# Scans with a PSUM operand, other first tiles and another order of a tile's matmul groups in a fused attention and expert kernel

## The chip, the core and the metric

The kernel runs on one core of one Trainium2 chip. The metric is the device time of one execution in microseconds (us). PE is TensorE (PEld its weight loads), DVE is VectorE, ACT is ScalarE, POOL is GpSimd, SP is SyncE, which issues nearly all DMAs.

## The reference

Three layers follow one another. The first is attention with a decaying state, for 4 batches, 8 heads, 768 steps and 48 channels:

```python
for t in range(S):
    state = alpha[:, :, t, :, None] * state + np.einsum('bhd,bhe->bhde', k[:, :, t], v[:, :, t])
    y[:, :, t] = np.einsum('bhd,bhde->bhe', q[:, :, t], state)
```

Its 3072 rows of 384 numbers then go through a mixture of eight experts: each row goes to the expert with the highest cosine similarity to `expert_emb` (divided by `tau`) and is weighted by the softmax's share of that expert. A dense layer with ELU (384 to 2048 to 384) ends the program. All of it is float32.

## The kernel before

**Tiles.** Attention runs over 24 tiles, numbered i: six chunks of 128 steps, and in each chunk the four batches. A tile holds all eight heads as four pairs (`NP`); a pair's two heads of 48 channels lie on partitions 0 to 47 and 64 to 111 (`C2` = 112 rows). The decays of a tile (`at`) are one row of four segments of `TP` = 129 values, 517 in all (`SW`). Four `at` and four `qk` buffers and five `vt` buffers rotate, so tile i + 4 is loaded into the buffer of tile i. The code works as follows; lines are those of the profile.

- `stR` (L340): one DVE scan from right to left gives R, the product of the decays from each step to the tile's end. Its second operand `back` is a row in SBUF that holds a floor, and 1.0 at each segment's end. A reciprocal (L341) puts 1/R of each segment's first step into the row `fore`. POOL makes Kh = k times R (L343).
- `stA` (L350): a second scan, of `at` with `fore`, gives A, the inverse factor of each step. POOL makes Qh = q times A (L352).
- `stS` (L380), "scores": 16 matmuls of Kh and Qh, 48 rows each, into two PSUM tiles. `stP` (L387): DVE multiplies each of the two with a triangle, which gives P.
- `stT` (L364): four transposes of Kh, copied by ACT to Kt (L367).
- `stC`: from chunk 1 on 16 matmuls of the carried state G with Qh ("state's share", L402, 48 rows by 64 columns); 16 of v with P ("values", L405, 128 rows by 64 columns), both into the one PSUM tile psY, which ACT copies to yT (L407); from chunk 1 on two matmuls with the identity that carry G over (L412); and 16 of Kt with v ("state's products", L415, 128 by 64) which make the next state. In the last chunk there is no next state, so L364, L412 and L415 are missing for tiles 20 to 23.
- `stG` copies the new state out of PSUM (ACT, L423), `stH` scales it by the tile's decay (ACT, four of L433).
- `stD` (L446): eight matmuls with `rhsX` give the tile's rows and the products with the normalized expert embeddings; ACT copies them (L459) and sums squares (L462), DVE reduces the products (L451, kept in the list `late`).
- Routing: six `GROUPS` of tiles go through some 29 small DVE instructions each (`stR1`, `stX`, `gates`, `stR2`), handed out twelve to a tile from the list `todo`; rows are then scaled by ACT and scattered by POOL's indirect DMA (`put`, L556).

**Order.** `fast()` is written out by hand (`manual_schedule`): each engine executes its instructions in the order of the code. In iteration i of the loop PE gets: scores of i + 1, transposes of i + 1, `stD` of i - 1, state's share, values, carry, state's products of i. DVE gets R of i + 2, P of i + 1 (first half), A of i + 2, P of i + 1 (second half), then small instructions. ACT gets the copies in the order in which the code names them, with `stE` (L356, a copy of eight values of A that waits for the scan) ahead of the copy of psY.

**Start.** Before the loop, SP issues the loads of tiles 0 to 3, of v for three tiles, of the constants, of `emb` (after tile 1) and of `sel`. PE multiplies ones eleven times (`warm`, L285), and tiles 0 and 1 are prepared. The embeddings' inverse norm is 11 small DVE instructions in `todo`; the scaled embeddings (L675) are transposed (L725, eT) in iteration 1, ahead of the first `stD`, which therefore is done for tiles 0 and 1 together in iteration 2.

After the loop, `ending()` finishes tiles 22 and 23, routes the last groups, and the experts' layers (`moe1`, L956 on) and the dense layer (`moe2`, L1144 on) follow; the change touches neither.

PSUM has eight banks: two for psX, three for the scores and the new state (psG), and one each for psT, psY and psR.

Of the kernel before, what the change touches and what calls it, by code (L numbers as in the profile page):

```python
# [8 lines left out]
F32 = mybir.dt.float32  # L9
# [17 lines left out]
TP = T + 1  # L27
SW = H // 2 * TP + 1
# [20 lines left out]
A_FLOOR = 1e-15  # L49
# [12 lines left out]
def fused_kernel(ctx, tc, qk, a, v, emb, w12, wi, wo, cst, sel, cols, out):  # L62
# [64 lines left out]
    def inv_norm1(pool, x):  # L127

        shape = [x.shape[0], 1]
        y = pool.tile(shape, F32, name="rs_y1")  # L130
        t = pool.tile(shape, F32, name="rs_t1")
        h = pool.tile(shape, F32, name="rs_h1")
        yi = y.bitcast(I32)
        steps = [
            lambda: nc.vector.tensor_scalar(yi, x.bitcast(I32), 1, None, op0=ALU.logical_shift_right),
            lambda: nc.vector.tensor_scalar(h, x, -0.5, None, op0=ALU.mult),
            lambda: nc.vector.tensor_scalar(yi, yi, -1.0, float(0x5F3759DF), op0=ALU.mult, op1=ALU.add),
        ]
# [5 lines left out]
        steps += [  # L144
            lambda: nc.vector.tensor_scalar(y, y, x, 1e-6, op0=ALU.mult, op1=ALU.add),
            lambda: nc.vector.reciprocal(y, y),
        ]
        return y, steps

# [137 lines left out]
    def attention():  # L287
        with ExitStack() as st:
# [15 lines left out]
            back = gp.tile([C2, SW], F32, name="back")  # L304
            fore = [gp.tile([C2, SW], F32, name=f"fore{i}") for i in range(2)]
# [4 lines left out]

            def seg(t, n=TP):

                return t[:, :NP * TP].rearrange("c (p t) -> c p t", t=TP)

# [17 lines left out]
            def stR(i):  # L332
# [10 lines left out]
                nc.gpsimd.tensor_tensor(Kh[i], qkt[i][:, 1], R[:, 1:].rearrange("c (p t) -> c p t", t=TP)[:, :, 1:], op=ALU.mult)  # L343

            def stA(i):
# [4 lines left out]
                nc.vector.tensor_tensor_scan(A, at.pop(i), fore[i % 2], 0.0, op0=ALU.mult, op1=ALU.add)  # L350
                Qh[i] = wk.tile([C2, NP, T], F32, bufs=3, name="Qh")
                nc.gpsimd.tensor_tensor(Qh[i], qkt.pop(i)[:, 0], seg(A)[:, :, 1:], op=ALU.mult)  # L352

            def stE(i):
                if i < NT:
                    nc.scalar.activation(out=chk[:, i], in_=seg(As.pop(i))[:, :, 0:TP:T], func=AF.Copy)  # L356

# [31 lines left out]
            yT = {}  # L389

            def stC(i):
                if i < 0 or i >= NT:
                    return
                cc, b = divmod(i, B)
                vv = vt[i % VB]
                y = psG.tile([128, NP, T], F32, tag="g", name="psY") if i == NT - 1 else ps1.tile([128, NP, T], F32, name="psY")
                pp, qh = P.pop(i), Qh.pop(i)
                if cc:
                    for p in range(NP):
                        for h2 in range(2):  # L400
                            rows = slice(HP * h2, HP * h2 + D)
                            nc.tensor.matmul(y[HP * h2:HP * (h2 + 1), p], G[b][rows, p], qh[rows, p], start=(p == 0), stop=False)  # L402
                for p in range(NP):
# [4 lines left out]
                if cc < NC - 1:  # L408
                    u = psG.tile([C2, NP, D], F32, tag="g", name="psU")
                    kk = Kt.pop(i)  # L410
                    if cc:
                        nc.tensor.matmul(u, c["ident"][:C2, :C2], G[b][:, :, :D], start=True, stop=False)  # L412
# [3 lines left out]
                    U_[i] = u  # L416
# [8 lines left out]
            def stH(i):  # L425
# [4 lines left out]
                if i >= B:  # L430
                    g = G[i % B]
                    for p in range(NP):
                        nc.scalar.activation(out=g[:, p, :D], in_=g[:, p, :D], func=AF.Copy, scale=seg(r)[:, p, 1:2])  # L433
# [5 lines left out]
            def stD(i, keep=False):  # L439
# [4 lines left out]
                x = psD.tile([128, NP, 128], F32, name="psX")  # L444
# [73 lines left out]

            def stR2(g):
# [3 lines left out]
                r = ps1.tile([128, 8, E], F32, tag="psT" if g == NG - 2 else "psR", name="psR")[:, :n]  # L523
# [50 lines left out]
            def general():  # L574
# [15 lines left out]
                with tc.For_i(0, NC, 1) as cc, tc.For_i(0, T // TB, 1) as tb:  # L590
                    ts = bass.ds(tb * TB, TB)
                    for b in range(B):
                        for p in range(NP):
                            for h2 in range(2):
                                p0 = (b * H + 2 * p + h2) * EG
                                ch = slice(h2 * HP, h2 * HP + D)
                                for nm, src in (("a", a[bass.ds(cc, 1), ch, b, bass.ds(tb * TB + (p * TP + 1), TB)]),
# [38 lines left out]
            def fast():  # L636
# [14 lines left out]
                warm(ps1, "psY", 11)  # L651
                nc.scalar.activation(out=warm_t, in_=ones, func=AF.Exp)
                nc.vector.memset(back, A_FLOOR)
                nc.vector.memset(back[:, 1:].rearrange("c (p t) -> c p t", t=TP)[:, :, T:], 1.0)
                nc.vector.memset(cum[:, 0], 0.0)
                for t in fore + G:
                    nc.gpsimd.memset(t, 0.0)
                zero = xp.tile([128, 1, XW], F32, tag="xt", name="zero")
                nc.gpsimd.memset(zero, 0.0)
                for j in range(2):  # L660
                    stR(j)
                    stA(j)
                    stE(j)
                    stH(j)
                rows, rtau = emb_t[:, :2 * NP * HP], emb_t[:, 2 * NP * HP:]
                es = sm.tile([E, 1], F32, name="es")
                esq = wk.tile([E, 2 * NP * HP], BF16, bufs=1, tag="junk", name="esq")
                nc.scalar.activation(out=esq, in_=rows, func=AF.Square, accum_out=es)
                en, steps = inv_norm1(sm, es)
                stS(0)  # L670
                stT(0)
# [624 lines left out]
```

## Time and profile before

| | |
|---|---|
| median of 3 runs | 808.1 us (806.57 to 811.5) |
| the profiled execution | 807.42 us |
| its span in the trace | 805.6 us |
| busy, share of the span: PE, DVE, ACT, POOL | 96%, 67%, 44%, 24% |

Times in the trace are counted from the span's start. What is called S0 to S23 below is the start of PE's weight loads for the scores of that tile (L380): each marks a tile. A wait is printed behind an instruction in brackets, with its length and what ended it.

### The profile page before, as it was taken

The page shows a single profiled execution, that of the slowest core. Times are in us where ns is not written, and L with a number is a line of the kernel's source. Part 1 is how long each engine was busy: PE and PEld are TensorE (multiplying, and loading weights), DVE is VectorE, ACT ScalarE, POOL GpSimd, SP SyncE. Part 2 cuts the span into 40 slices and gives each one's busy share as a digit, 9 for nine tenths or more (in the row PEclk, how much of TensorE's full clock was granted, in tenths as well). Part 3 has the DMA queues.
Part 4 walks back from the last instruction along what each step waited for, and adds up shares of the span by engine and source line. Part 5 has one row for each costly group of instructions (what it writes and reads, how often), then busy time and mean ns, then how long its engine had stood idle before and what let it go on. Part 6 is the DMA issues. An engine that isn't in the chain of part 4 may idle for free.

```text
span 805.6 us, 13707 instructions
## 1 busy us (share of the span) xinstructions
PE 774.2 (96%) x5064; PEld 700.7 (87%) x5064; DVE 538.6 (67%) x1015; ACT 358.0 (44%) x783; POOL 190.1 (24%) x218
## 2 busy tenths in 40 slices
PE   7799998889999999999999999999999999999996
PEld 5688877669999999999988899999999999999996
DVE  7779999956877788888467665454545545545442
ACT  2466877624554555555355443333333333323331
POOL 6433656612333343343000020010002002002002
PEclk7899999999999999999999999999999999999999
DMA  9988863266656557563000010000001001000001
GB/s 246 255 237 216 229 182 95 109 196 157 194 184 206 179 193 231 173 213 111 1 0 1 2 40 1 0 11 31 1 1 39 1 1 40 0 1 30 11 1 39
DMA packets 44805, 77.72 MB, mean 96 GB/s; under 512 B 11958, under 2 KB 18230, under 8 KB 44734
## 3 DMA queue, kind: packets, MB, share of 16 engines
q1 hardware_dynamic: 41662, 67.36, 28.9%
q0 software_dynamic: 3072, 9.45, 3.2%
q8 instruction: 40, 0.66, 0.4%
q14 instruction: 31, 0.25, 0.1%
HBM read 64.58 MB, written 12.22 MB: 95 GB/s over the span
## 4 chain that ended last, share of the span: by engine, by line
PE 39%; issue 30%; DVE 3%; POOL 2%; ACT 2%; POOLq 0%; ACTq 0%
PE h L1144 6%; PE y L988 5%; PE y L990 4%; PE y L989 4%; PE h L957 4%; PE h L958 4%; PE h L956 4%; POOL out_dram L1178 2%; PE o L1167 2%; PE o L1165 2%; PE o L1166 2%; PE t L937 1%; DVE dlo L260 1%; DVE g L1150 1%; DVE mn L1146 1%
## 5 line engine op out<-in xcount | busy, mean ns | idle before, releaser
L1146 DVE TENSOR_SCALAR mn<-h 128x512 f32<-128x512 f32 x96 | 66.2, 690 | 139.7 <-PE h L1144 139.7
L1147 ACT ACTIVATE mn<-mn 128x512 f32<-128x512 f32 x96 | 60.7, 633 | 171.9 <-DVE mn L1146 171.9
L1167 PE MATMUL o<-dwo,gl 128*128 128x384 f32 x384 | 129.4, 337 | 1.4 <-DVE gl L1154 1.4
L1166 PE MATMUL o<-dlo,gh 128*128 128x384 f32 x384 | 128.4, 334 | 0.0
L1165 PE MATMUL o<-dwo,gh 128*128 128x384 f32 x384 | 128.2, 334 | 0.0
L1144 PE MATMUL h<-xh,dwi 128*128 128x512 f32 x288 | 112.8, 391 | 0.6 <-ACT x2T L1002 0.6
L1144 PE MATMUL h<-xh,dlo 128*128 128x512 f32 x288 | 113.2, 393 | 0.0
L1144 PE MATMUL h<-xl,dwi 128*128 128x512 f32 x288 | 112.5, 392 | 0.0
L1178 POOL DMA_INDIRECT out_dram<-ob,ids x24 | 23.2, 966 | 341.8 <-ACT ob L1175 338.1
L1153 ACT ACTIVATE gh<-g 128x512 fp32r<-128x512 f32 x96 | 60.7, 633 | 77.6 <-DVE g L1150 77.6
L960 ACT ACTIVATE hh<-h 128x432 fp32r<-128x432 f32 (+6 forms) x64 | 32.4, 507 | 106.2 <-PE h L958 99.1
L204 DVE TENSOR_TENSOR wlo<-raw,whi 128x512 fp32r<-128x512 f32 x96 | 73.2, 789 | 5.6 <-ACT whi L201 4.8
L1150 DVE SCALAR_TENSOR_TENSOR g<-mn,h 128x512 f32<-128x512 f32 x96 | 66.1, 688 | 15.2 <-ACT mn L1147 14.7
L1165 PEld LDWEIGHTS o<-dwo,gh 128*128 128x128 f32 x384 | 72.0, 187 | 4.2
L1166 PEld LDWEIGHTS o<-dlo,gh 128*128 128x128 f32 x384 | 72.0, 187 | 4.0
L1167 PEld LDWEIGHTS o<-dwo,gl 128*128 128x128 f32 x384 | 72.2, 188 | 2.1 <-DVE gl L1154 1.7
L961 DVE SCALAR_TENSOR_TENSOR hl<-h,hh 128x432 fp32r<-128x432 f32 (+6 forms) x64 | 36.7, 573 | 47.6 <-ACT hh L960 46.2
L988 PE MATMUL y<-hh,whi 128*128 128x432 f32 (+6 forms) x192 | 68.4, 356 | 0.0
L956 PE MATMUL h<-xh,whi 128*128 128x432 f32 (+6 forms) x192 | 66.5, 346 | 0.7 <-ACTq L1015 0.7
L244 POOL TENSOR_SCALAR dg<-dg 128x384 f32<-128x384 f32 x32 | 42.0, 1312 | 106.3 <-ACT dg L243 106.2
L1154 DVE TENSOR_TENSOR gl<-g,gh 128x512 fp32r<-128x512 f32 x96 | 65.7, 684 | 1.2 <-ACT gh L1153 1.1
L958 PE MATMUL h<-xh,wlo 128*128 128x432 f32 (+6 forms) x192 | 66.4, 346 | 0.0
(210 smaller groups left out, 1520.5 us busy)
## 6 DMA issues: line engine op xcount, KB each, us to landing
raw<-in_w_dram SPq DMA_DIRECT2D x96, 256.0 KB, 3.3
qk<-in_qk_dram SPq DMA_DIRECT2D x40, 192.0 KB, 3.9
vt<-in_v_dram SPq DMA_DIRECT2D x24, 256.0 KB, 4.7
raw<-in_wi_dram SPq DMA_DIRECT2D x16, 384.0 KB, 4.3
raw<-in_wo_dram SPq DMA_DIRECT2D x16, 384.0 KB, 4.1
xr<-xs SPq DMA_DIRECT2D x7, 576.0 KB, 4.9
at<-in_alpha_dram SPq DMA_DIRECT2D x40, 96.9 KB, 3.0
xs<-zero SPq DMA_DIRECT2D x7, 288.8 KB, 5.5
```

The lines of the kernel that those rows point to most:

```text
L204: nc.vector.tensor_tensor(l[:, sl], r, h[:, sl].bitcast(F32), op=ALU.subtract)
L956: nc.tensor.matmul(ps, wh, xh[:, kk], start=(kk == 0), stop=False)
L958: nc.tensor.matmul(ps, wl, xh[:, kk], start=False, stop=(kk == KD - 1))
L988: nc.tensor.matmul(acc[e][d], wh, hh, start=(f == 0), stop=False)
L1144: nc.tensor.matmul(ps, l, x, start=(n == 0), stop=(n == len(terms) - 1))
L1146: nc.vector.tensor_scalar(mn, ps, 0.0, None, op0=ALU.min)
L1147: nc.scalar.activation(out=mn, in_=mn, func=AF.Exp)
L1150: nc.vector.scalar_tensor_tensor(g, mn, -1.0, ps, op0=ALU.add, op1=ALU.max)
L1154: low.append(lambda: nc.vector.tensor_tensor(gl, g, gh.bitcast(F32), op=ALU.subtract))
L1165: nc.tensor.matmul(o_, gh[:, sl], wh, start=(f == 0), stop=False)
L1166: nc.tensor.matmul(o_, gh[:, sl], wl, start=False, stop=False)
L1167: nc.tensor.matmul(o_, gl[:, sl], wh, start=False, stop=(f == M - 1))
```

## The change

**PSUM operand.** One PSUM bank `pz` is set aside; its first column holds the floor (2^-50 in place of 1e-15), and both scans take it, broadcast along the row, as their second operand; `back` and `fore` are gone. Each segment gets three leading values (0, 1/floor, 1) and a trailing 1/floor, so that the scan comes to 1 by itself; a tile's row is 528 values long. The reciprocal goes into the third leading value of `at`. Since psR has no bank any more, its users move: eT and the counts of the first groups to psX, the count of group 4 stays in psT, the last one and the check's sum go into `pz`.

**First tiles.** `emb` is loaded ahead of tile 1. There are 20 warm matmuls and 4 more behind the transposes of tile 0. The inverse norm is split: two DVE instructions (`first`), 14 on ACT (`steps`), a DVE reciprocal in iteration 0 between P and A, and two scalings on ACT; eT follows in iteration 0, and `stD` of tile 0 in iteration 1. Three bf16 constants are made in iteration 3, on ACT and POOL, and no longer ahead of the loop on DVE.

**Order.** `stC` is cut in three: `stC_state` (L402), `stC_carry` (the tile psU and L412) and `stC_values` (L405, L407, L415). PE's order in iteration i becomes: scores of i + 1, state's share of i, transposes of i + 1, `stD` of i - 1, carry of i, values of i, state's products of i. Where `stR2` is due, the reductions in `late` come ahead of it.

The diff, cut to its core:

```diff
+LEAD = 3
+TP = LEAD + T + 1
+SW = NP * TP
...
-A_FLOOR = 1e-15
+A_FLOOR = 2.0 ** -50
@@ inv_norm1 @@
+        first = [
+            lambda: vec.tensor_scalar(yi, x.bitcast(I32), 1, None, op0=ALU.logical_shift_right),
+            lambda: vec.tensor_scalar(yi, yi, -1.0, float(0x5F3759DF), op0=ALU.mult, op1=ALU.add),
         ]
+        steps = [lambda: act.activation(out=h, in_=x, func=AF.Copy, scale=-0.5)]
         for _ in range(3):
             steps += [
-                lambda: nc.vector.scalar_tensor_tensor(t, y, h, y, op0=ALU.mult, op1=ALU.mult),
-                lambda: nc.vector.scalar_tensor_tensor(y, t, 1.5, y, op0=ALU.add, op1=ALU.mult),
+                lambda: act.activation(out=t, in_=y, func=AF.Copy, scale=h),
+                lambda: act.activation(out=t, in_=t, func=AF.Copy, scale=y),
+                lambda: act.activation(out=t, in_=t, func=AF.Copy, bias=1.5),
+                lambda: act.activation(out=y, in_=t, func=AF.Copy, scale=y),
             ]
+        steps += [lambda: act.activation(out=y, in_=y, func=AF.Copy, scale=x, bias=1e-6)]
@@ attention @@
-            back = gp.tile([C2, SW], F32, name="back")
-            fore = [gp.tile([C2, SW], F32, name=f"fore{i}") for i in range(2)]
+            pz_p = st.enter_context(tc.tile_pool(name="pz", bufs=1, space=PS))
+            pz = pz_p.tile([128, 512], F32, name="pz")
+            floor = pz[:C2, 0:1].to_broadcast([C2, SW])
@@ stR, stA @@
-                nc.vector.tensor_tensor_scan(R[:, ::-1], at[i][:, ::-1], back[:, ::-1], 0.0, op0=ALU.mult, op1=ALU.max)
-                nc.vector.reciprocal(seg(fore[i % 2])[:, :, 0:1], seg(R)[:, :, 1:2])
+                nc.vector.tensor_tensor_scan(R[:, ::-1], at[i][:, ::-1], floor, A_FLOOR, op0=ALU.mult, op1=ALU.max)
+                nc.vector.reciprocal(seg(at[i])[:, :, LEAD - 1:LEAD], seg(R)[:, :, LEAD:LEAD + 1])
...
-                nc.vector.tensor_tensor_scan(A, at.pop(i), fore[i % 2], 0.0, op0=ALU.mult, op1=ALU.add)
+                nc.vector.tensor_tensor_scan(A, at.pop(i), floor, 0.0, op0=ALU.mult, op1=ALU.max)
@@ stC @@
             def stC(i):
+
+                stC_state(i)
+                stC_carry(i)
+                stC_values(i)
...
+                if cc < NC - 1:
+                    U_[i] = psG.tile([C2, NP, D], F32, tag="g", name="psU")
+                    if cc:
+                        nc.tensor.matmul(U_[i], c["ident"][:C2, :C2], G[b][:, :, :D], start=True, stop=False)
@@ stR2 @@
-                r = ps1.tile([128, 8, E], F32, tag="psT" if g == NG - 2 else "psR", name="psR")[:, :n]
+                r = count_tile(g)[:, :n]
@@ fast, before the loop @@
                 load(0)
                 nc.sync.dma_start(out=cs, in_=cst)
+                nc.sync.dma_start(out=emb_t, in_=emb)
                 load(1)
                 load_v(0)
-                nc.sync.dma_start(out=emb_t, in_=emb)
...
-                warm(ps1, "psY", 11)
+                warm(ps1, "psY", 20)
...
+                nc.vector.memset(pz[:, 0:1], A_FLOOR)
...
                 for j in range(2):
                     stR(j)
                     stA(j)
-                    stE(j)
                     stH(j)
+                    if j == 0:
+                        stE(j)
+                        nc.scalar.activation(out=esq, in_=rows, func=AF.Square, accum_out=es)
                 stS(0)
                 stT(0)
+                warm(ps1, "psY", 4)
+                for f in guess:
+                    f()
+                nc.vector.reciprocal(rtau, rtau)
+                stE(1)
                 stP(0, 0)
                 stP(0, 1)
-                todo.extend([lambda: nc.vector.reciprocal(rtau, rtau)] + steps
-                            + [lambda: nc.vector.tensor_scalar(rows, rows, en, rtau, op0=ALU.mult, op1=ALU.mult)])
-                nc.vector.tensor_tensor(strict16, c["tri"], c["ident"], op=ALU.subtract)
-                nc.vector.tensor_copy(ident16, c["ident"])
-                nc.vector.tensor_copy(base16[:, 0], c["base"])
+                for f in newton:
+                    f()
@@ the loop @@
                     stS(i + 1)
+                    stC_state(i)
                     stT(i + 1)
                     if i - 3 in last:
+                        while late:
+                            late.pop(0)()
                         todo[:0] = stR2(last[i - 3])
                     stR(i + 2)
                     stP(i + 1, 0)
+                    if i == 0:
+                        nc.vector.reciprocal(en, en)
+                        nc.scalar.activation(out=rows, in_=rows, func=AF.Copy, scale=en)
+                        nc.scalar.activation(out=rows, in_=rows, func=AF.Copy, scale=rtau)
                     stA(i + 2)
                     stP(i + 1, 1)
...
-                    if i == 2:
-                        stD(0)
-                    if i > 1:
+                    if i > 0:
                         stD(i - 1)
+                    stC_carry(i)
                     stE(i + 2)
-                    stC(i)
-                    if i == 1:
-                        step(len(todo))
-                        eT = ps1.tile([128, NP, E], F32, tag="psR", name="eT")
+                    stC_values(i)
+                    if i == 0:
+                        eT = psD.tile([128, NP, E], F32, tag="psX", name="eT")
                         for p in range(NP):
                             nc.tensor.transpose(eT[:, p], rows[:, p * 128:(p + 1) * 128], c["ident"][:E, :E])
-                        nc.vector.tensor_copy(rhsX[:, :, CW:CW + E], eT)
+                        nc.scalar.activation(out=rhsX[:, :, CW:CW + E], in_=eT, func=AF.Copy)
+                    if i == 3:
+                        nc.scalar.activation(out=ident16, in_=c["ident"], func=AF.Copy)
+                        nc.scalar.activation(out=base16[:, 0], in_=c["base"], func=AF.Copy)
+                        nc.gpsimd.tensor_tensor(strict16, c["tri"], c["ident"], op=ALU.subtract)
```

## Rows read from the trace of the kernel before

**Rows 1.** Windows by stage: stretch, busy us of each engine (instructions), PEclk, DMA, GB/s.

```profile
0.00:45.49 45.49, 34.42 (x345) 28.15 (x345) 34.49 (x60) 16.86 (x49) 21.90 (x26) 0.81 0.95 247
45.49:147.04 101.55, 95.35 (x1310) 80.71 (x1308) 95.57 (x198) 71.79 (x228) 56.12 (x59) 1.00 0.66 186
...
171.95:805.60 633.65, 623.91 (x3247) 578.04 (x3246) 386.73 (x625) 258.13 (x473) 100.91 (x113) 1.00 0.22 70
```

**Rows 2.** Timeline of PE's weight loads over one tile: start us, length us, instruction.

```profile
45.49 0.97 PEld L380 LDWEIGHTS psS<-Qh,Kh 48*128 48x128 f32 x16
46.58 0.39 PEld L364 LDWEIGHTS psT<-cs,Kh 112*128 112x128 f32 x4
46.93 0.97 PEld L446 LDWEIGHTS psX<-rhsX,yT 128*128 128x128 f32 x8
48.00 0.85 PEld L402 LDWEIGHTS psY<-Qh,G 48*64 48x64 f32 x16
49.02 0.85 PEld L405 LDWEIGHTS psY<-P,vt 128*64 128x64 f32 x16 [0.17 <-issue]
50.05 0.27 PEld L412 LDWEIGHTS psU<-G,cs 112*112 112x112 f32 x2 [0.17 <-issue]
50.56 0.54 PEld L415 LDWEIGHTS psU<-vt,Kt 128*64 128x64 f32 x16 [0.24 <-issue]
51.15 0.30 PEld L380 LDWEIGHTS psS<-Qh,Kh 48*128 48x128 f32 x4
```

**Rows 3.** The same timeline, tiles 0 and 1 of L446 behind one another.

```profile
28.09 3.53 PEld L446 LDWEIGHTS psX<-rhsX,yT 128*128 128x128 f32 x16
```

**Rows 4.** Timeline of DVE and POOL in the tile of rows 2.

```profile
46.69 0.69 DVE L387 TENSOR_TENSOR P<-psS,cs 128x512 f32<-128x512 f32 x1 [1.26 <-PE psS L380]
47.29 1.23 DVE L350 TENSOR_TENSOR_SCAN A<-at,fore 112x517 f32<-112x517 f32 x1
48.44 0.67 DVE L387 TENSOR_TENSOR P<-psS,cs 128x512 f32<-128x512 f32 x1
48.66 1.19 POOL L352 TENSOR_TENSOR Qh<-qk,A 112x512 f32<-112x512 f32 x1 [2.14 <-DVE A L350]
...
49.11 1.83 DVE L340 TENSOR_TENSOR_SCAN R<-at,back 112x517 f32<-112x517 f32 x1
```

**Rows 5.** DVE's groups from 45.49 to 147.04 us: count | busy us, mean ns | idle.

```profile
L350 DVE TENSOR_TENSOR_SCAN A<-at,fore 112x517 f32<-112x517 f32 x17 | 31.5, 1852 | 0.0
...
L340 DVE TENSOR_TENSOR_SCAN R<-at,back 112x517 f32<-112x517 f32 x16 | 20.9, 1306 | 0.0
```

**Rows 6.** Timeline of DVE and POOL at the start.

```profile
4.00 1.23 DVE L340 TENSOR_TENSOR_SCAN R<-at,back 112x517 f32<-112x517 f32 x1 [2.20 <-DMA at<-in_alpha_dram]
...
7.72 2.10 POOL L352 TENSOR_TENSOR Qh<-qk,A 112x512 f32<-112x512 f32 x1
```

**Rows 7.** Timeline of PE's weight loads, three waits.

```profile
9.87 1.78 PEld L380 LDWEIGHTS psS<-Qh,Kh 48*128 48x128 f32 x16 [4.81 <-POOL Qh L352]
...
25.12 0.32 PEld L725 LDWEIGHTS eT<-cs,emb_t 8*128 8x128 f32 x4 [3.38 <-DVE emb_t L675]
...
145.98 0.97 PEld L446 LDWEIGHTS psX<-rhsX,yT 128*128 128x128 f32 x8 [1.49 <-ACT yT L407]
```

**Rows 8.** One window of 4 us at the start, columns as in rows 1.

```profile
8.00:12.00 4.00, 2.13 (x17) 1.91 (x18) 2.79 (x4) 0.82 (x3) 4.00 (x3) 0.54 1.10 271
```

**Rows 9.** Timeline of DVE: a product with both operands in SBUF.

```profile
79.32 0.65 DVE L204 TENSOR_TENSOR wlo<-raw,whi 128x512 fp32r<-128x512 f32 x1
```

**Rows 10.** ACT's groups from 45.49 to 147.04 us, columns as in rows 5.

```profile
L433 ACT ACTIVATE G<-G,R 112x48 f32<-112x48 f32 x71 | 17.7, 323 | 0.0
L407 ACT ACTIVATE yT<-psY 128x512 f32<-128x512 f32 x17 | 10.0, 591 | 5.9 <-PE psY L405 5.8
...
L356 ACT ACTIVATE chk<-A 112x8 f32<-112x8 f32 x17 | 3.5, 205 | 10.5 <-DVE A L350 10.5
```

**Rows 11.** The DMA view of the first 40 us: GB/s in 40 slices.

```profile
GB/s 0 14 246 305 282 315 297 279 274 281 247 283 342 302 252 285 282 215 186 237 259 225 207 262 246 217 271 360 344 292 253 241 333 287 260 192 265 177 164 262
```

More of the change, by code (lines that the diff above doesn't have):

```diff
@@ L394, in stC @@
                 cc, b = divmod(i, B)
-                vv = vt[i % VB]
-                y = psG.tile([128, NP, T], F32, tag="g", name="psY") if i == NT - 1 else ps1.tile([128, NP, T], F32, name="psY")
-                pp, qh = P.pop(i), Qh.pop(i)
+                y = ys[i] = psG.tile([128, NP, T], F32, tag="g", name="psY") if i == NT - 1 else ps1.tile([128, NP, T], F32, name="psY")
+                qh = Qh.pop(i)
                 if cc:
@@ L402, in stC, with stC_carry, stC_values @@
                             nc.tensor.matmul(y[HP * h2:HP * (h2 + 1), p], G[b][rows, p], qh[rows, p], start=(p == 0), stop=False)
+            def stC_carry(i):
+                if i < 0 or i >= NT:
+                    return
+                cc, b = divmod(i, B)
+                if cc < NC - 1:
+                    U_[i] = psG.tile([C2, NP, D], F32, tag="g", name="psU")
+                    if cc:
+                        nc.tensor.matmul(U_[i], c["ident"][:C2, :C2], G[b][:, :, :D], start=True, stop=False)
+            def stC_values(i):
+                if i < 0 or i >= NT:
+                    return
+                cc, b = divmod(i, B)
+                vv, pp, y = vt[i % VB], P.pop(i), ys.pop(i)
                 for p in range(NP):
@@ L408, in stC @@
                 if cc < NC - 1:
-                    u = psG.tile([C2, NP, D], F32, tag="g", name="psU")
+                    u = U_[i]
                     kk = Kt.pop(i)
-                    if cc:
-                        nc.tensor.matmul(u, c["ident"][:C2, :C2], G[b][:, :, :D], start=True, stop=False)
                     for p in range(NP):
@@ L432, in stH @@
                     for p in range(NP):
-                        nc.scalar.activation(out=g[:, p, :D], in_=g[:, p, :D], func=AF.Copy, scale=seg(r)[:, p, 1:2])
+                        nc.scalar.activation(out=g[:, p, :D], in_=g[:, p, :D], func=AF.Copy, scale=seg(r)[:, p, LEAD:LEAD + 1])
             xt, lg = {}, {}
@@ L443, in stD @@
                 y = yT.pop(i)
-                x = psD.tile([128, NP, 128], F32, name="psX")
+                x = psD.tile([128, NP, 128], F32, tag="psX", name="psX")
                 for p in range(NP):
@@ L517, in gates, with count_tile @@
                 ]
+            def count_tile(g):
+                if pz is None:
+                    return ps1.tile([128, 8, E], F32, tag="psR", name="psR")
+                if g == NG - 1:
+                    return pz[:, 64:64 + 8 * E].rearrange("p (n e) -> p n e", e=E)
+                if g == NG - 2:
+                    return ps1.tile([128, 8, E], F32, tag="psT", name="psR")
+                return psD.tile([128, 8, E], F32, tag="psX", name="psR")
             def stR2(g):
@@ L596, in general @@
                                 ch = slice(h2 * HP, h2 * HP + D)
-                                for nm, src in (("a", a[bass.ds(cc, 1), ch, b, bass.ds(tb * TB + (p * TP + 1), TB)]),
+                                for nm, src in (("a", a[bass.ds(cc, 1), ch, b, bass.ds(tb * TB + (p * TP + LEAD), TB)]),
                                                 ("k", qk[bass.ds(cc, 1), ch, b, 1, p, ts]),
@@ L650, in fast @@
                 nc.vector.memset(ones, 1.0)
-                warm(ps1, "psY", 11)
+                warm(ps1, "psY", 20)
                 nc.scalar.activation(out=warm_t, in_=ones, func=AF.Exp)
-                nc.vector.memset(back, A_FLOOR)
-                nc.vector.memset(back[:, 1:].rearrange("c (p t) -> c p t", t=TP)[:, :, T:], 1.0)
+                nc.vector.memset(pz[:, 0:1], A_FLOOR)
                 nc.vector.memset(cum[:, 0], 0.0)
-                for t in fore + G:
+                for t in G:
                     nc.gpsimd.memset(t, 0.0)
@@ L659, in fast @@
                 nc.gpsimd.memset(zero, 0.0)
+                rows, rtau = emb_t[:, :2 * NP * HP], emb_t[:, 2 * NP * HP:]
+                es = sm.tile([E, 1], F32, name="es")
+                esq = wk.tile([E, 2 * NP * HP], BF16, bufs=1, tag="junk", name="esq")
+                en, guess, newton = inv_norm1(sm, es)
                 for j in range(2):
@@ L751, in decays @@
                 g2 = sm.tile([C2, 1], F32, name="g2")
-                t = ps1.tile([1, 1], F32, tag="psR", name="psB")
+                t = pz[:1, 256:257]
                 d = chk[:, :, :, 1:2].rearrange("p n a o -> p (n a) o")
@@ L777, in ending @@
                 stP(i + 1, 1)
+                late.pop(0)()
                 r = stR2(g2 - 1)
@@ L1240, in _layout @@
     heads(inputs["k"], 0.0, qk[:, :, :, 1])
[L1241 to L1244 removed]
+    steps = np.empty((NC, C2, B, NP, TP), np.float32)
+    heads(inputs["alpha"], 1.0, steps[..., LEAD:LEAD + T])
+    steps[..., :LEAD] = 0.0, 1.0 / A_FLOOR, 1.0
+    steps[..., LEAD + T] = 1.0 / A_FLOOR
+    al = steps.reshape(NC, C2, B, SW)
     vv = np.zeros((NC, T, B, NP, VW), np.float32)
```

38 lines of the change are left out of this document (10 added, 28 removed).

## The prediction

> **What bounds the kernel now.** I read the windows by stage first [rows 1]. From 171.95 us on PE is busy 623.91 of 633.65 us, and the change adds and removes nothing there; it only starts that stage earlier or later. What counts is when S23 begins, 147.04 us, since the 24.91 us from there to 171.95 (the ending) keep their order. In 45.49 to 147.04 us (S6 to S23, 17 periods) PE is busy 95.35 and DVE 95.57 of 101.55 us at full clock: both are near their limit, ACT (71.79) and POOL (56.12) are not. In 0 to 45.49 us PE is busy 34.42 us at a mean granted clock of 0.81, and the DMA engines 0.95 of the time.
>
> Next, the timeline of one undisturbed tile [rows 2]: S6 at 45.49, the next scores at 51.15, so 5.66 us, with PE never waiting for another engine. The reader should look at the ends: the weight loads of one group end and those of the next begin 0.12, 0, 0.10, 0.17, 0.18, 0.24 and 0.05 us later. The zero is between transposes and L446, both on the whole array, and two L446 behind one another take 3.53 us for 16, an even 0.22 each at the low clock, without a seam [rows 3]. A gap stands where the shape in rows and columns changes.
>
> Then DVE beside POOL [rows 4]: A takes 1.23 us alone, R takes 1.83 us when Qh (1.19) has begun 0.45 us before it, while P, with one operand in PSUM, keeps its 0.67 beside the same Qh. So a scan with two operands in SBUF waits for POOL, and a product with one in PSUM does not. Over the 17 periods A means 1.852 us and R 1.306 [rows 5]. It works the other way too: the first Qh takes 2.10 us beside a scan [rows 6].
>
> **The steady tiles, S6 to S23.** Scans: what the waits cost is 17 x (1.852 - 1.23) + 16 x (1.306 - 1.23) = 11.8 us of DVE. A scan becomes 528/517 longer (1.256), and reading PSUM is not shown for a scan; the nearest rows are P, 0.67, and a product with both operands in SBUF, 0.65 [rows 4, 9], so 0.02 more: 1.28, for 33 scans 1.7 us. Bounds: 1.25, and 1.83 if the operand changes nothing. DVE's need becomes 95.57 - 11.8 + 1.7 = 85.5 us.
>
> [...]
>
> Order: in the new sequence the carry follows L446 (whole array both) and state's products follow values (128 by 64 both), so six changes of shape become four. The six gaps sum to 0.86 us; two of average size are 0.29, I take 0.25, with the ends 0 and 0.35. It applies to 14 of the 17 tiles, since tiles 20 to 23 have no carry and no products: 3.5 us. PE's need: 95.35 - 3.5 = 91.85 us, now clearly above DVE's.
>
> PE's idle time there was 101.55 - 95.35 = 6.2 us, where DVE was late: behind batches of small instructions, and ahead of tile 21's L446, where PE waited 1.49 us for yT [rows 7]. That last wait stays, since L446 follows the eviction directly at the loop's end. Of the other 4.7 us I keep a quarter, 1.2, because DVE's need drops to 93% of PE's. So 91.85 + 2.7 = 94.55 instead of 101.55: **7.0 us**. Ends: 9.7 if no idle is left, 0 if neither part works.
>
> **The first tiles, S0 to S6.** The first decays land and R of tile 0 starts at 4.00 [rows 6]; that stays. Four scans of 1.28 with two reciprocals put the end of A of tile 1 at about 9.75, its Qh at 11.05, S1 at 11.1. S0 moves from 9.87 [rows 7] to about 8.2, as Qh of tile 0 loses its 0.9 us of waiting. DVE then has the three small instructions (0.4), both P of tile 0 to 11.5, R of tile 2 to 12.8 and P of tile 1 to 13.6. Now comes the added wait: the reciprocal of the norm stands on DVE ahead of A of tile 2, and behind it wait A, P and every later scan. It needs 14 dependent ACT instructions, which start at about 10.7, behind Kt of tile 0 and the copy of A. Nearest rows: 0.205 us for eight values, 0.323 with a scale per partition, four of which overlap [rows 10]. Ten have such a scale: 10 x 0.3 + 4 x 0.2 = 3.8, done at 14.5 (ends 2.8 and 4.5, so 13.5 and 15.2). A of tile 2 starts at 14.7 instead of 13.6. Kt of tile 1 and yT of tile 0 queue behind the chain on ACT; their users, state's products of tile 1 and L446 of tile 0, come after 18 us.
>
> From A on: 1.28, POOL's start 0.14, Qh 1.19 [rows 4], PE's start 0.05 (Qh of tile 0 ends at 9.82, S0 follows at 9.87 [rows 6, 7]), so 2.66: S2 at 17.35. A period is then the loop scores to P 1.2, to A 0.6 [rows 2, 4], and the 2.66 just summed: 4.46 us, above PE's tile in the first chunk (5.66 less L402, 1.02, L412, 0.51 and a seam: 4.0). S3 21.8, S4 26.3, S5 30.7, and with the first carried state a tile of 5.41: S6 at 36.1 instead of 45.49: **9.4 us** (8.5 to 10.3). What goes: the embeddings' wait of 3.38 us at 25.12 [rows 7], the double L446, and the low clock, 0.54 in 8 to 12 us [rows 8], behind a wait of 4.81 us. In the new order no gap in the first 18 us is longer than about 1.5 us, with 20 warm matmuls before S0 and four behind T, so I keep full clock from there.
>
> Loads: DMA is saturated, so this start must still be fed. By the tiles' sizes `at` of tile 4 ends at 4.2 MB, of tile 7 at 7.4 MB (fill 0 of 0.69 MB ahead of it). The moved rates reach 4.2 MB at about 17 us and 7.4 at about 29 [rows 11]; the scans want them at 20.5 and 34. On SP the early `emb` is 16 KB and 0.4 us of issue; the loads of tiles 4 to 8 are issued earlier, since A and Qh free the buffers earlier. 3 us of cover; if it is gone, the start gains that much less.
>
> **At nothing:** the three constants in iteration 3 (0.4 us on ACT, 0.4 on POOL, needed in iteration 8); counts in the psX ring (its other tile's readers are done an iteration earlier, the reductions in `late` being put ahead); the missing fills of `back` and `fore`. **Added:** L402 now comes right behind the scores and needs psY free. Values end 0.5 us ahead of the next scores (the length of the products), the eviction takes 0.59 [rows 10] and a start of 0.1, and L402 stands 1.09 behind the scores' start [rows 2]: 0.9 us of cover, which holds while ACT is on time; its mean need is 71.79 / 17 = 4.2 of 5.41 us a tile. I charge 0.3 us.
>
> **Sum:** 9.4 + 7.0 - 0.3 = 16.1. The profiled span 805.6 becomes 789.5, with the 1.8 around it 791.3; the median of the runs stood 0.7 above this execution, so **792.0 us**.
>
> **Rivals.**
> 1. ACT takes DVE's place: L402 waits for yT, the carry for the copy of the old state. For: the cover is 0.9 us, one buffer. Against: ACT is busy 71.79 of 101.55 [rows 1]. 0.3 us in 15 tiles: 4.5 more, 796.5.
> 2. The start keeps half of its loss: the clock falls once (at half clock a tile's 4.0 us become 8, some 3.5 more than the loop), or ACT's chain or the loads are late: 4.6 more, 796.6.
> 3. The order saves nothing: shapes that differ in rows alone, scores and share, cost as much as all others and the two pairs keep their seams: 3.5 more, 795.5.
> 4. Two of these together: 800 to 801.
> 5. Slower than before: the broadcast PSUM operand slows the scan itself. Each 0.1 us adds 3.3 us of DVE in the steady part and about 1 us at the start; PE's lead over DVE (6.4) and the gain (16.1) are used up at about 1.8 us a scan. At 2.0 us, a little above the 1.83 of rows 4, it would be some 817 us. For: no row shows such a scan. Against: P reads 512 values from PSUM in 0.67 and a scan takes twice that per value anyway. That the operand changes nothing (the lock stays) is the same case at 1.83 beside POOL only: it leaves the start and the order, about 799.
>
> **Chances.** The forecast 0.54, rival 1 0.15, rival 2 0.12, rival 3 0.08, rival 4 or the lock 0.07, slower 0.04. The range: down to 785, with ACT's chain at its low end (0.9), no idle left (2.7), seams at 0.35 (1.4), and 2 us for the spread of runs (806.57 to 811.5); up to 800, where rivals 1 to 3 lie. About 1% (8 us, below 800 or above 816) is what a measurement of this kernel tells from no change: faster 0.88, same 0.08, slower 0.04.
>
> **What would show it.** Scans at 1.25 to 1.3 us everywhere, beside POOL too; Kh and Qh at 1.18 from tile 0; one tile at about 5.4 us with no seam between L446 and the carry and between values and products; full clock from about 5 us; S2 near 17, S6 near 36, S23 near 131. Wrong would be: PE waiting for yT or for the copy of the state behind the scores, DVE waiting for ACT longer than 2 us before A of tile 2, or R waiting for a load in tiles 3 to 8.

## The result, and the profile after

| | before | after |
|---|---|---|
| median of 4 runs each | 807.4 us (806.57 to 811.5) | 795.4 us (793.91 to 798.72) |
| ratio, 95% interval | | 0.983 (0.9805 to 0.986) |
| the profiled execution, its span | 807.42, 805.6 us | 796.37, 794.6 us |
| S6, S23 | 45.49, 147.04 us | 39.03, 134.77 us |
| weight loads of the first expert | 171.95 us | 159.73 us |

The changed kernel has its own line numbers: R is L340, A L350, Kh L343, Qh L352, scores L380, state's share L407, transposes L364, `stD`'s products L463, carry L416, values L425, state's products L433, the scatter of `put` L583. The four stages of its trace, columns as in [rows 1]:

```profile
0.00:39.03 39.03, 32.63 (x359) 25.88 (x359) 27.67 (x46) 21.14 (x65) 20.12 (x25) 0.91 0.98 250
39.03:134.77 95.74, 91.87 (x1310) 81.35 (x1308) 85.78 (x202) 72.42 (x230) 56.64 (x60) 0.98 0.82 213
134.77:159.73 24.96, 20.32 (x167) 13.74 (x166) 21.34 (x130) 11.17 (x36) 10.58 (x21) 1.00 0.40 132
159.73:794.60 634.87, 624.01 (x3247) 578.05 (x3246) 386.74 (x625) 258.34 (x473) 101.50 (x113) 1.00 0.23 70
```

The start, up to S6, gives 6.46 us (45.49 less 39.03) and the steady tiles, S6 to S23, 5.8 (101.55 less 95.74); the ending takes as long as before (24.96 us, 24.91 before), the experts 1.2 us more (634.87, 633.65 before): 11.0 us of the span. DVE's need (its busy time, which the stretch can't go below) fell from 95.57 to 85.78, PE's only from 95.35 to 91.87, and the granted clock of the second row is 0.98, not 1.00.

One undisturbed tile of the changed kernel, PE's weight loads, answers [rows 2]:

```profile
44.36 0.97 PEld L380 LDWEIGHTS psS<-Qh,Kh 48*128 48x128 f32 x16
45.45 0.85 PEld L407 LDWEIGHTS psY<-Qh,G 48*64 48x64 f32 x16
46.48 0.39 PEld L364 LDWEIGHTS psT<-cs,Kh 112*128 112x128 f32 x4 [0.17 <-issue]
46.82 0.97 PEld L463 LDWEIGHTS psX<-rhsX,yT 128*128 128x128 f32 x8
47.72 0.28 PEld L416 LDWEIGHTS psU<-G,cs 112*112 112x112 f32 x2
48.23 0.85 PEld L425 LDWEIGHTS psY<-P,vt 128*64 128x64 f32 x16 [0.24 <-issue]
49.05 0.60 PEld L433 LDWEIGHTS psU<-vt,Kt 128*64 128x64 f32 x16
49.70 0.41 PEld L380 LDWEIGHTS psS<-Qh,Kh 48*128 48x128 f32 x6
```

It takes 5.34 us (5.66 before). The carry begins before the loads of L463 have ended, and state's products before those of values have: those two seams are gone, and four gaps are left.

The scans beside POOL, a tile earlier, answer [rows 4] (a line of three dots stands for lines left out, here as in the code below):

```profile
40.83 1.24 DVE L350 TENSOR_TENSOR_SCAN A<-at,pz 112x528 f32<-112x528 f32 x1
...
42.15 1.28 POOL L352 TENSOR_TENSOR Qh<-qk,A 112x512 f32<-112x512 f32 x1 [2.17 <-DVE A L350]
...
42.67 1.24 DVE L340 TENSOR_TENSOR_SCAN R<-at,pz 112x528 f32<-112x528 f32 x1
```

R begins 0.5 us behind Qh, as in [rows 4], and takes what A takes alone.

Two stretches went otherwise than forecast. The first is at S2, where the forecast kept full clock. PE's weight loads there answer [rows 7], the windows under them [rows 8]:

```profile
16.69 0.32 PEld L759 LDWEIGHTS eT<-cs,emb_t 8*128 8x128 f32 x4 [1.95 <-ACT emb_t L731]
17.62 1.76 PEld L380 LDWEIGHTS psS<-Qh,Kh 48*128 48x128 f32 x16 [0.61 <-POOL Qh L352]
...
20.22 1.83 PEld L463 LDWEIGHTS psX<-rhsX,yT 128*128 128x128 f32 x8
...
24.78 0.97 PEld L380 LDWEIGHTS psS<-Qh,Kh 48*128 48x128 f32 x16
```

```profile
14.86:17.62 2.76, 0.41 (x6) 0.32 (x5) 2.74 (x4) 2.66 (x7) 1.27 (x1) 1.00 1.04 245
17.62:24.78 7.16, 7.16 (x60) 6.70 (x61) 4.29 (x7) 2.28 (x6) 3.81 (x3) 0.52 1.06 230
```

PE was busy for 0.41 of 2.76 us, then the granted clock was 0.52 in the mean of the tile, and PE was busy all of it: 7.16 us where the next period, at 1.00, took 4.45.

The second is at S14. POOL's timeline, last Qh ahead of the first scatter and Kh behind it:

```profile
74.95 1.28 POOL L352 TENSOR_TENSOR Qh<-qk,A 112x512 f32<-112x512 f32 x1 [0.62 <-DVE A L350]
79.22 1.14 POOL L583 DMA_INDIRECT xs<-xt,pos_i  x1 [2.99 <-DMA at<-in_alpha_dram]
...
81.65 1.28 POOL L343 TENSOR_TENSOR Kh<-qk,R 112x512 f32<-112x512 f32 x1
```

The scatter started 2.99 us late, Kh and Qh of tile 14 behind it, PE waited 1.8 us for S14, and the clock fell again behind that wait (0.75 from 84.20 to 91.13 us): S13 to S15 took 14.01 us, two tiles take 10.67. So 3.3 us went here; 1.0 of them came back by S23, where the stretch is 2.3 us longer than in the kernels below that lack this wait (95.74 and 93.4). The row names a load of `at` as what ended the wait; the scatter doesn't read `at`, and the experiments show another cause.

### The profile page after: what moved, and what is told of

Read it like the earlier page. It is cut to its first block, busy times and chain, and to the rows that moved or that the text cites. A ratio compares the mean times of both kernels' runs of the same rounds, so it can differ in the third digit from the quotient of the medians.

```text
span 794.6 us, 13699 instructions
## 1 busy us (share of the span) xinstructions
PE 768.8 (97%) x5077; PEld 699.0 (88%) x5077; DVE 521.5 (66%) x1001; ACT 363.1 (46%) x802; POOL 188.8 (24%) x217
## 4 chain that ended last, share of the span: by engine, by line
PE 38%; issue 30%; DVE 3%; POOL 3%; ACT 2%; DMA 1%; POOLq 0%; SPq 0%; ACTq 0%
PE h L1184 6%; PE y L1028 5%; PE y L1030 4%; PE y L1029 4%; PE h L998 4%; PE h L996 4%; PE h L997 4%; POOL out_dram L1218 2%; PE o L1207 2%; PE o L1205 2%; PE o L1206 2%; PE t L977 1%; DVE dlo L259 1%; DVE g L1190 1%; DVE mn L1186 1%
```

## The experiments

All of e1 to e10 are compared with runs of the kernel before on the same chip, where it took 809.9 to 810.3 us; so ratios are compared, and the stages of the traces. Scores still mark a tile; columns from S2 on are in us.

| run | ratio to before (95%) | S2 | S3 | S6 | S13 to S15 | S23 | S6 to S23 |
|---|---|---|---|---|---|---|---|
| before | 1 | 18.70 | 25.46 | 45.49 | 11.46 | 147.04 | 101.55 |
| after, first profile | 0.983 (0.9805 to 0.986) | 17.62 | 24.78 | 39.03 | 14.01 | 134.77 | 95.74 |
| e7 after again | 0.980 (0.978 to 0.982) | 17.73 | 24.73 | 38.99 | 11.49 | 133.81 | 94.82 |
| e1 order alone | 0.9985 (0.997 to 1.000) | 18.70 | 25.45 | 45.15 | 12.12 | 145.92 | 100.77 |
| e2 order undone | 0.985 (0.983 to 0.987) | 17.57 | 23.14 | 37.71 | 11.32 | 134.30 | 96.59 |
| e3 floor in SBUF | 0.9975 (0.996 to 0.999) | 18.96 | 24.54 | 39.32 | 12.58 | 143.21 | 103.89 |
| e4 PE filled | 0.981 (0.979 to 0.983) | 17.54 | 22.00 | 36.24 | 16.71 | 135.16 | 98.92 |
| e5 POOL padded | 0.9795 (0.977 to 0.982) | 17.73 | 22.19 | 36.44 | 10.67 | 129.85 | 93.41 |
| e6 both | 0.977 (0.975 to 0.979) | 17.69 | 22.14 | 36.39 | 10.67 | 129.79 | 93.40 |
| e8 both, late reduction first | 0.9755 (0.9735 to 0.9775) | 17.44 | 21.90 | 36.14 | 10.67 | 129.57 | 93.43 |
| e9 as e8, not filled | 0.978 (0.975 to 0.980) | 18.02 | 25.13 | 39.37 | 10.67 | 132.80 | 93.43 |
| e10 as e9, four warm fewer | 0.976 (0.974 to 0.978) | 17.55 | 22.01 | 36.26 | 10.68 | 129.69 | 93.43 |

**e1, the order alone**, on the kernel before:

```
 stS(i + 1)
+stC_state(i)
 stT(i + 1)
 ...
+stC_carry(i)
 stE(i + 2)
-stC(i)
+stC_values(i)
```

> Only the new order of the matmul groups, on the kernel before: scans with two SBUF operands, the old start, counts in their own buffer. Theory (the order takes its seams from PE, and pays only where PE is the bound): one undisturbed tile falls from 5.66 to about 5.33 us where DVE keeps up, but DVE's need from S6 to S23 stays at 95.6 us, so the stretch falls from 101.55 to 98 to 100 and the time to 804 to 806. Rival (the two parts add up freely): 14 tiles x 0.33 = 4.6 us, 802.8. Rival (the order saves nothing by itself): 807.4.

**e2, the order undone**, on the changed kernel: the same lines the other way round, the carry again between values and state's products.

> The changed kernel with the old order of a tile's groups (state's share, values, carry, products in one piece at the end). Theory: each of the 14 full tiles gets its two shape changes back, 0.33 us each as the undisturbed tiles show (5.66 against 5.335), so 4.6 us: S6 to S23 about 100, time near 800. S6 stays at about 39. Rival (the scans alone made the tile shorter, the order nothing): 795.4, tile 5.33.

The windows S6 to S23 of e1 and, below, of e2:

```profile
45.15:145.92 100.77, 90.64 (x1310) 79.91 (x1308) 95.54 (x200) 72.49 (x230) 57.12 (x59) 1.00 0.68 188
```

```profile
37.71:134.30 96.59, 95.07 (x1310) 80.70 (x1308) 87.38 (x201) 71.69 (x228) 56.74 (x59) 1.00 0.80 215
```

The tile is 5.33 us in e1 and 5.66 in e2, so the order is worth 0.33 us a tile by itself, and PE's need falls by 4.7 us with it (95.35 to 90.64). But e1's stretch is only 0.8 us shorter, less than the 1.5 to 3.5 that the theory had: DVE's need stands at 95.54. Part of that miss is a wait of 0.8 us ahead of e1's first scatter, of the kind that e5 treats below: S13 to S15 took 0.66 us more than before, so without it the order alone would bring some 1.4 us (an estimate). The time of e1 is 0.15% lower (95% interval 0 to 0.3%), 1.2 us, where the theory had 1.4 to 3.4.

In e2 the scans alone bring 5.0 us, with PE at 95.07 of 96.59. The theory had a stretch of about 100 us, since it added 4.6 us to the 95.74 of the changed kernel; but e2 has no wait for the scatter, and a shorter stretch at the low clock (0.95 granted up to S6, 0.91 in the changed kernel; S2 to S3 5.57 us, S6 at 37.71). So in the time, too, it loses less than 4.6 us to the changed kernel. Together, without the scatter's wait (e5), the two parts make the stretch 8.14 us shorter, more than 0.8 (or 1.4) and 5.0. It lasts as long as the larger of the two needs and some idle time, 4 to 6 us where DVE's need is the larger (before, e1, e3) and 1.5 to 3 where PE's is (e2, e5, e6).

**e3, the operand in SBUF**, all else as in the changed kernel:

```
-floor = pz[:C2, 0:1].to_broadcast([C2, SW])
+fl = gp.tile([128, 1], F32, name="fl")
+floor = fl[:C2, 0:1].to_broadcast([C2, SW])
```

> The changed kernel with one thing put back: the constant operand of the scans lies in SBUF (one value per partition, broadcast) instead of PSUM. Theory (two SBUF operands make a scan and a POOL product wait for one another): scans beside a product take 1.8 us or more again, DVE's need from S6 to S23 rises from 85.8 to about 97 and becomes the bound, the stretch takes 99 to 103 us, S6 comes 1 to 3 us later, time 800 to 805. [...] Rival (scan with PSUM pays extra, hidden so far): scans shorter than 1.24 us, time below 795.

DVE's timeline in a tile of e3, and the window S6 to S23:

```profile
41.12 1.52 DVE L351 TENSOR_TENSOR_SCAN A<-at,fl 112x528 f32<-112x528 f32 x1
...
43.24 1.87 DVE L341 TENSOR_TENSOR_SCAN R<-at,fl 112x528 f32<-112x528 f32 x1
```

```profile
39.32:143.21 103.89, 90.74 (x1311) 79.91 (x1309) 99.98 (x200) 72.83 (x230) 60.42 (x59) 1.00 0.69 198
```

One value per partition, broadcast from SBUF, brings the wait back (1.87 us for this R, and 1.88 in the mean for A, instead of 1.24). DVE's need is 99.98 and sets the stretch, 2.3 us longer than before. So the gain of the steady tiles hangs on this one operand. The gain of the start doesn't: S6 comes at 39.32, so 6.2 us are kept (0.3 us less than in the changed kernel, 1.6 less than in e2, whose stretch at the low clock is as short as here). They are lost again in the steady tiles and in the ending, which takes 28.32 us here (24.91 before), with PE waiting 2.2 us for the reduction that e8 treats and a low clock behind it (state's share 1.97 us, then 1.09); what else is in these 3.4 us was not tried. The time is 0.9975 of that before. The shortest scan of e3 takes 1.244 us, against 1.231 in the changed kernel: no price of reading PSUM shows.

**e4, PE filled**, on the changed kernel:

```
+warm(psD, "psX", 7)
 eT = psD.tile(...)
 ...
+warm(psD, "psX", 2)
```

> The changed kernel with nine more matmuls of no use (0.21 us each) while PE waits between the products of tile 0 and the scores of tile 2, 14.9 to 17.6 us: seven before the transposes of the embeddings, two behind them. Theory (the clock falls at S2 because PE had waited): S2 stays at 17.6 at full clock, S3 comes at 21.8 to 22.3 instead of 24.8, S6 at 36 to 36.5, time 2.5 to 3 us lower, about 792.6. Rival (the period of 7.2 us is a wait for ACT or a load, and the clock only follows): S3 at 24.8 again, 795.4.

S3 came at 22.00 and S6 at 36.24, as the theory says, and then all was given back in this execution: S13 to S15 took 16.71 us, since the first scatter was 4.20 us late, PE waited 2.88 us for S14, and the clock fell behind that (state's share 1.97 us, 1.09 a tile earlier). The ratio, 0.981, is that of the changed kernel (0.980 and 0.983); the theory had 2.5 to 3 us less. S15 came at 91.05 us, as in the changed kernel (91.13), which looked like a transfer that both waited for. POOL's scatter in e4:

```profile
77.63 1.15 POOL L583 DMA_INDIRECT xs<-xt,pos_i  x1 [4.20 <-ACT Kt L367]
```

Here the row names a copy by ACT as what ended the wait, in the changed kernel a load: the scatter uses neither.

**e5, POOL padded; e6, both; e7, the changed kernel again; e8, the reduction first.** In five kernels' traces (the changed kernel and its repeat e7, e1, e3, e4) the first scatter started 2.1 to 2.6 us behind a packet of 8 KB on the queue that carries instructions. The scatter's place among POOL's instructions (those that only wait for a semaphore included) separates the kernels; times are in us:

| | place | packet at | Qh ends | scatter starts |
|---|---|---|---|---|
| before | 80 | 74.2 | 84.8 | 85.02 |
| e2 | 79 | 69.4 | 76.4 | 76.58 |
| e5, e6 | 80 | 63.0, 64.4 | 73.6, 73.6 | 73.81, 73.76 |
| after, e7 | 72 | 76.6, 75.9 | 76.2, 76.2 | 79.22, 78.24 |
| e1 | 73 | 82.5 | 83.9 | 84.69 |
| e3 | 72 | 77.3 | 78.8 | 79.63 |
| e4 | 72 | 75.0 | 73.4 | 77.63 |

The edit of e5, which e6, e8, e9 and e10 have too:

```
 nc.gpsimd.memset(zero, 0.0)
+for _ in range(8):
+    nc.gpsimd.memset(tick, 0.0)
```

Expected of e5:

> The changed kernel with eight one-value memsets more on POOL at about 2.3 us, where it waits for the first loads. In the four kernels with the wait, the first scatter is POOL's 72nd or 73rd instruction of the kernel and starts 2.0 to 2.6 us behind an 8 KB packet of the instruction queue; in the two without it (before, and the order undone) it is the 80th and 79th, and the packet came 7 to 11 us ahead of it. Theory (the scatter waits for POOL's own instructions to be fetched, at a time when the DMA engines are full): as 80th it starts 0.2 us behind Qh, S14 and S15 come 5.3 us after one another, S15 at 87.8 instead of 91.1, and the time is 3.3 us lower than that of the changed kernel on the same chip. Rival (the scatter waits for a fill or a load, or for the full DMA engines as such): it starts at 79.2 again, no change of the time. S3 stays at 24.8.

Of e6, which has the nine matmuls of e4 as well:

> The nine matmuls in PE's first waits and the eight memsets on POOL together. Theory (the start's 3 us were won in the run with the matmuls alone, and lost again because the scatter's wait grew from 3.0 to 4.2 us and the clock fell behind it): S6 at 36.2, S14 and S15 at 5.3 us each, S23 at about 129, time 6 us below the run with the matmuls alone, ratio to before about 0.973. Rival (the loads are the bound at that place: S15 came at 91.1 us in both kernels): S15 at 90 to 91 again, with DVE's R or POOL's Kh waiting for at or qk, ratio 0.98.

Of e7:

> The changed kernel itself on this chip, to compare the others with. Same ratio to before as in the first runs, 0.983; S3 at 24.8 and the scatter's wait of 3 us again if both belong to the program and not to one execution; else S3 near 22 or S14 and S15 at 5.3 us in this profile.

POOL's timeline of e6, the same two instructions as in the changed kernel's:

```profile
72.31 1.28 POOL L352 TENSOR_TENSOR Qh<-qk,A 112x512 f32<-112x512 f32 x1 [0.62 <-DMA qk<-in_qk_dram]
73.76 1.40 POOL L583 DMA_INDIRECT xs<-xt,pos_i  x1 [0.17 <-DMA vt<-in_v_dram]
```

Eight memsets at the start, when POOL waits anyway, took the wait away in all five kernels that have them (0.16 or 0.17 us left in e5, e6 and e8): S14 and S15 follow at 5.33 us. Loads, fills and the full DMA engines (share 1.05 in e8 from S13 to S15) are the same, so the rival falls. What is shown is that the wait hangs on the scatter's place in POOL's program. That POOL waited there for its own instructions is the reading that fits the place and the packets; the trace doesn't name the engine that a packet belongs to. Full DMA engines, which the theory had as a condition, did not last through the delay behind the packet: in e1 their share was about 0.2 in its first half microsecond (82.5 to 83 us), and the scatter still started 2.1 us behind it. Whether they hold up the packet itself was not tried.

e7 had the scatter's wait (2.06 us) and the low clock at S2 again (0.91 granted up to 36 us, S2 to S3 7.00 us), so both belong to the program, if not to each execution. In e5 the clock held at S2 (1.00 granted up to S6), where S3 was expected at 24.8, though nothing was filled and PE waited as long as in the changed kernel:

```profile
16.81 0.32 PEld L761 LDWEIGHTS eT<-cs,emb_t 8*128 8x128 f32 x4 [2.00 <-ACT emb_t L733]
17.73 0.97 PEld L380 LDWEIGHTS psS<-Qh,Kh 48*128 48x128 f32 x16 [0.61 <-POOL Qh L352]
```

The times gained less than expected. e5's median is 1.3 us below that of e7 on the same chip (792.51 and 793.82), not 3.3, and the intervals of their ratios overlap. e6 has a ratio of 0.977, not 0.973, about 3 us below e4 and not 6. The 3.3 us were read from one stretch of one execution, before the 1.0 us that came back, and of e7's five runs the profiled one, with the wait, was the slowest (796.19; the others 792.83 to 794.26).

Expected of e8:

> As the kernel with both repairs, and in the ending the small reduction that frees the buffer of the counts stands ahead of the two masked products on DVE instead of behind them. Theory (the ending is bound by DVE's chain of small instructions): the 1.5 us that PE waits there for the reduction go, but S23 to the first expert stays at 24.9 or falls by 0.4 at most. Rival (PE's wait is on the path): 1.3 to 1.5 us less than the kernel with both repairs.

Its edit in the ending, on e6:

```
+late.pop(0)()
 stP(i + 1, 0)
 stP(i + 1, 1)
-late.pop(0)()
```

PE in the ending of e6, where the reduction (L468) stands behind both P:

```profile
132.43 0.19 PE L552 MATMUL psR<-base,ident 128*128 128x32 bf16 x1 [1.47 <-DVE lg L468]
...
132.67 1.34 PE L407 MATMUL psY<-Qh,G 48*64 48x128 f32 x16
133.94 1.98 PE L425 MATMUL psY<-P,vt 128*64 128x128 f32 x16
```

The same place in the changed kernel's first profile:

```profile
137.41 0.19 PE L552 MATMUL psR<-base,ident 128*128 128x32 bf16 x1 [1.48 <-DVE lg L468]
...
138.68 1.09 PE L425 MATMUL psY<-P,vt 128*64 128x128 f32 x16
```

S23 to the first expert took 26.28 us in e6 and 25.03 in e8, the size that the rival named, and e8's median is 1.6 us below e6's. But the changed kernel's first profile has the same wait (1.48) and 24.96 us: there the clock held (1.00 granted in that stage). In e6 it fell behind the wait (0.94 in that stage, values 1.98 us, else 1.09), as in e5 and e7 (26.2 and 26.6). So the wait cost nothing by itself, as the theory has it, and some 1.3 us where the clock fell.

**e9 and e10, less to do for PE at the start**: e9 is e8 without the nine matmuls of e4, and e10 is e9 without the four matmuls behind the transposes of tile 0.

> The kernel with all three edits, without the nine matmuls in PE's waits of 14.9 to 17.6 us. What it tells: the clock fell at S2 in two profiles of the changed kernel, did not with the nine matmuls, and did not in the one profile with the eight memsets alone. Theory (the waits make the fall likely, and the matmuls prevent it): in some executions S3 comes 2.5 to 3 us later, the mean granted clock of the five runs is 0.994 to 0.997 instead of 0.998, the median 0.5 to 2 us above the kernel with all three, and the runs spread over 2 us or more. Rival (the fall is chance and the matmuls do nothing): ratio 0.9755 to before and runs within 1.3 us, as with them.

> As the kernel just described, and the four matmuls behind the transposes of tile 0 (1.03 us of PE) are taken out too, so that PE waits about 1.7 us instead of 0.7 ahead of S1. Theory (more waiting, a surer fall): the clock is low in part of 8 to 24 us in this profile, S3 at 24 or later, time 2 to 4 us above the kernel with all three edits. Rival (the waits have nothing to do with it): S3 near 22 and the time of the kernel with all three.

Windows of e10, from T of tile 1 to S2 and from S2 to S3:

```profile
13.00:17.55 4.55, 4.12 (x46) 3.58 (x42) 3.50 (x6) 4.27 (x13) 2.54 (x2) 0.62 1.06 245
17.55:22.01 4.46, 4.05 (x60) 3.71 (x60) 3.79 (x6) 2.46 (x8) 2.55 (x2) 1.00 1.04 237
```

e9 had the low clock at S2 again (0.50 from 18 to 24 us, S2 to S3 7.11 us), and its median is 1.8 us above that of e8, which ran on another chip; its five runs have a mean granted clock of 0.994 to 0.996, those of e8 0.997 to 0.999. The ratios' intervals overlap, so this stands on the clocks and the traces. e10, whose theory had S3 at 24 or later and 2 to 4 us more, is the surprise: the clock did fall, earlier, between 13 and 17.55 us, where PE's values stretched to 1.97 us and still ended before S2, which ACT's chain and POOL set. Its clocks are those of e9 (0.994 to 0.996), its time is that of e8. The theory of e10 was wrong in its price: the low clock (0.62) cost nothing here, where PE waited for others, while in the changed kernel (0.52), where PE set the pace, S2 to S3 took 7.16 us and not 4.46. What decides in which execution and where the clock falls, the runs don't settle. From S2 to S3 it held in the three traces with the nine matmuls (e4, e6, e8); of the seven other traces with the new start it fell in five (after, e7, e9, and for a shorter time in e2 and e3) and held in two (e5, e10). That fits the theory that the filling prevents the fall, and with so few executions doesn't show it.

## Why the prediction was right, and where its steps were not

The time fell into the range, 3.4 us above the forecast of 792.0, by terms that missed both ways. The time alone would fit rivals 1 to 3 as well (796.5, 796.6 and 795.5); the traces tell them apart.

**Scans: right.** 1.24 us was measured, 1.28 forecast, beside POOL too. That DVE's need came out at 85.78 against 85.5 is in part luck: the 33 scans took 41.0 us where 42.2 were forecast, and DVE's other instructions 1.6 us more than before, which the forecast had not. The rival of a slower scan is ruled out: the shortest scan takes 1.231 us with the operand in PSUM and 1.244 with it in SBUF (e3), so the 0.02 us that the forecast added for PSUM does not show. That a scan with both operands in SBUF waits beside POOL's product, e3 shows again (1.87 us), here for an input of one value per partition.

**Order: right in kind, too small.** 0.33 us a tile (e1, e2) in place of 0.25. That it saves anything rules out rival 3. At full clock PE's need is 90.36 (e6) against 91.85 forecast; that the first profile has 91.87 is chance, since it holds matmuls at the lower clock (0.98 in that row). Idle time was 3.0 us (93.40 less 90.36), forecast 2.7. The stretch without the scatter's wait is 93.4, forecast 94.55.

**First tiles: the working was right, one step failed.** S2 17.62 (17.35 forecast), period 4.45 (4.46), S6 36.1 to 36.4 wherever the clock held (36.1 forecast). S1 came at 11.69 and not 11.1, since DVE waited 1.17 us for the decays of tile 1 to land, which the forecast had not charged; S2 hung on ACT's chain and hardly moved. The step that failed is "no gap in the first 18 us is longer than about 1.5 us", so "I keep full clock": PE waited 1.95 us for the embeddings and 0.61 for Qh, and the clock fell. The prediction's own times held such a gap: S1 at 11.1 and the four groups of tile 1 and tile 0 behind it (1.09, 0.35, 1.03 and 0.59 in [rows 2]) end at 14.2, and up to S2 at 17.35 only the four transposes of the embeddings stand between, which had to wait for ACT's chain (14.5) and two scalings on ACT (0.70 and 0.72 us in the trace) that the sum left out. The cost was 2.9 us at S6 (39.03 less 36.14 in e8): rival 2's mechanism, at 2.9 us instead of 4.6. The same gap with full clock in e5 shows that it makes the fall possible, not certain.

**At nothing: two effects were not nothing.** The first scatter moved from POOL's 80th place to the 72nd and waited there, most likely for its instructions: 3.3 us from S13 to S15 in the first profile, 2.3 by S23. The prediction has no term for this. Seven of the eight places are waits that fall away with the new order of the groups (e1, the order alone, has the scatter as 73rd; e2, without it, as 79th). The last is the sum of two fills less and one of the three constants more. No row of before shows the wait, since there the packet came 11 us early. And "the counts in the psX ring" with "the reductions in late being put ahead" added a wait of 1.5 us in the ending, whose order the prediction took as kept; it cost some 1.3 us where the clock fell behind it. Of ACT's lateness (0.3) nothing was seen: from S6 to S23 PE's weight loads wait once for yT, 1.0 us, at the place of the wait in [rows 7].

**The sum.** Forecast 9.4 + 7.0 - 0.3; in the first profile 6.46 + 5.8, and 1.2 lost among the experts. That last stretch took 633.5 to 634.9 us in the traces (633.65 before), and PE waited there 0.8 to 1.3 us for the rows of an expert in the traces of before, after and e1 to e4; it isn't put down to the change. So the 11.0 us of the span are the 16.1 forecast, less 2.9 at the start, 2.3 at the scatter and 1.2 among the experts, and some 1.4 more from the steady tiles (8.12 in e8, 6.7 forecast): misses that in part cancel, and to that part it is luck that the time lies in the range. With the three edits (e8) the parts are 9.35 and 8.12, the span is 16.8 us shorter than before (16.1 forecast), and the kernel is some 2.5% faster than before, 0.4 of a point more than the changed kernel on that chip (0.9755 against 0.980).

## What to carry to other kernels

Where two engines are near their limit, cost a change against both needs: PE's saving alone was worth 0.8 us (some 1.4 without the scatter's wait), on top of DVE's it was worth three. Look at what a wait on PE is followed by, not only at its length: a low clock cost 2.5 to 2.9 us at S2, where the next stretch was bound by PE, and nothing where PE waited anyway (e10). Filling such a wait with matmuls is worth a try. A change in one engine's order can shift the place of another engine's instructions in its program, and with it a stall that no dependence explains; here eight idle instructions earlier removed it (2.99 us in the first profile, 0.17 in e6).

## What the runs showed that was not expected

- POOL's first scatter waited 0.8 to 4.2 us, most likely for instructions, in the kernels where it is POOL's 72nd or 73rd, and 0.2 us as 79th or 80th.
- POOL's products take 1.27 us with rows of 132 values (1.28 in e3, so it isn't the operand in PSUM), 1.18 with rows of 129 (before, e1). Which part of the new layout does it was not tried.
- The granted clock fell behind PE waits of 1.5 to 2 us, in some executions and not in others: behind 1.95 us in the first profile (0.52 from S2 to S3), not behind 2.00 in e5 (1.00 up to S6).
